# Linear attention, then a routed MoE on one core: the routing table moved into the attention, one dispatch per expert

## Chip, cores and metric

The kernel runs on one core of a Trainium2 chip. The metric is device time in microseconds, the median of several executions. Durations of single instructions come from one profiled execution, whose own time is given with its span.

## What is computed

The reference, cut to what matters:

```python
for t in range(S):                       # q, k, v, alpha: (4, 8, 768, 48), f32
    state = alpha[:, :, t, :, None] * state + einsum('bhd,bhe->bhde', k[:, :, t], v[:, :, t])
    y[:, :, t] = einsum('bhd,bhde->bhe', q[:, :, t], state)
x = y.transpose(0, 2, 1, 3).reshape(3072, 384)
...
xn = x / (norm(x) + 1e-6); en = emb / (norm(emb) + 1e-6)
logits = xn @ en.T / tau                 # 8 experts
expert_idx = argmax(logits, axis=1)
probs = exp(logits - max); probs /= probs.sum() + 1e-9
gate_w = probs[arange(N), expert_idx]
for e in range(8):                       # w1[e]: 384x1024, w2[e]: 1024x384
    h = maximum(x[mask] @ w1[e], 0)
    out[mask] = gate_w[mask, None] * (h @ w2[e])
```

With the reference's seeded inputs the experts get 418, 365, 379, 426, 395, 371, 351 and 367 of the 3072 rows.

## The kernel before

The work is in three stages, each with tile pools of its own. A scheduler orders the instructions on each engine from the program order and the tiles' dependencies, so an instruction can stand earlier than its line suggests; each engine then runs its own list strictly in order.

**Attention** (lines 95 to 399). The 4 x 768 tokens are 24 chunks of 128; six chunks make a sequence. The eight heads are padded to 64 columns and lie two to a 128-wide pair. The loop at L383 is a software pipeline over chunks s: `load` (L223, SP's queue: alpha, k, q, v, four buffers), `decays` (L233: PE turns alpha, k and q into pa, pk and pq, L216; DVE scans r at L246 and a at L260, and makes kr at L253 and qs at L266), `scores` (L317: PE's sc, which DVE masks into sm at L330), `keys_back` (L268: pkb, copied to kb by ACT), `update` (L295: PE's pd, which DVE adds to the decayed state at L315, or copies at L311 in the first chunk of a sequence), `decay_state` (POOL's dec, L287), `mix_states` and `mix_chunk` (PE's py, L340 and L352, copied to yT by ACT at L358) and `rows` (L360: PE's px at L365 turns rows back to tokens and gives the logits; ACT copies x at L367; DVE sums the logits lg at L368; SP's queue stores the row to `x_rows` in DRAM at L373; ACT sums the squares). In one pass, `rows` works on chunk s-3, `mix_chunk` on s-2, `update` on s-1 and `decays` on s. The PSUM tiles py, px and pd share one pool, `ps_mm`, of three buffers (tag "mm", L100); a buffer is free again when the last reader of its tile is done. The three turned tiles have three buffers, sc has one: seven of eight banks.

After each sequence `choose(b)` (L182) takes the largest normed logit and the gate of its 768 rows: ACT's Sqrt (L187) and Exp (L204), 13 small DVE instructions, and six POOL adds that count how many earlier chunks' rows each partition gave to each expert (L201).

**Routing table** (lines 402 to 488). It begins when all chunks are chosen. Two matmuls give each row its rank within its expert (rk, L408 and L411), DVE turns the ranks to places in 128-row blocks, L450 to L453 build `put` (token number and gate, spread over the block numbers), and 24 matmuls (inv, L458) invert the placing. The result is, for each of at most 31 blocks, which token to gather (gidx), where to scatter (sidx), the gate (bgate), the block's expert (eblk) and whether it needs new weights (fresh).

**Experts** (lines 491 to 577). `block(j)` (L504) reads the expert's number into a register of SP, loads the 1.5 MB w1 and w2 of that expert into the buffer of parity j (skipped where the block two before had the same expert), gathers 128 rows (L524, an indirect DMA from POOL's queue), turns them (pxg, xgT), runs 24 matmuls of 128 columns for the first layer (ph, L543), with ACT's Relu, and 8 of 384 columns for the second (pyo, L553), multiplies by the gate on DVE (L557) and scatters the rows (L558). 24 blocks stand in a row. The number of further ones is read into a register of every engine (L571), and a `Switch` at L575 branches to an arm with that many blocks; here it is three.

```python
        ps_mm = c1.enter_context(tc.tile_pool(name="ps_mm", bufs=3, space=PSUM))
...
        more = nc.values_load(
            nmore, min_val=0, max_val=NBLK - NS,
...
        for n in tc.Switch(more, NBLK - NS + 1):
            for j in range(NS, NS + n):
                block(j)
```

Of the kernel before, what the change touches and what calls it, by code (L numbers as in the profile page):

```python
# [15 lines left out]
SP = mybir.EngineType.SP  # L16

# [6 lines left out]
def kernel(  # L24
# [24 lines left out]

    NBLK = (N + E * (P - 1)) // P  # L50
    FAR = 1 << 20

    x_rows = nc.dram_tensor("x_rows", (N, DM), FP32, kind="Internal").ap()
# [14 lines left out]
    cols_i = consts.tile([P, P], I32)  # L68
    nc.gpsimd.iota(cols_i, pattern=[[1, P]], base=0, channel_multiplier=0)
    cols = consts.tile([P, P], FP32)  # L70
# [6 lines left out]
    nc.vector.tensor_scalar(first, cols[:, 0:E], -1.0, float(E), ALU.mult, ALU.add)  # L77


    lg = consts.tile([P, NS, E], FP32)  # L80
    sq = consts.tile([P, NS], FP32)
    gate = consts.tile([P, NS], FP32)
    chosen = consts.tile([P, NS, E], FP32)
    before = consts.tile([P, NS + 1, E], FP32)
    nc.gpsimd.memset(before[:, 0], 0.0)
    rtau = consts.tile([P, 1], FP32)
    gidx = consts.tile([P, NBLK], I32)
    sidx = consts.tile([P, NBLK], I32)
    bgate = consts.tile([P, NBLK], FP32)
    eblk = consts.tile([1, NBLK], I32)  # L90
    fresh = consts.tile([1, NBLK], I32)
    nmore = consts.tile([1, 1], I32)


    with ExitStack() as c1:
        pads = c1.enter_context(tc.tile_pool(name="pads", bufs=1))
        work = c1.enter_context(tc.tile_pool(name="work", bufs=2))
        ps_tr = c1.enter_context(tc.tile_pool(name="ps_tr", bufs=3, space=PSUM))
        ps_sc = c1.enter_context(tc.tile_pool(name="ps_sc", bufs=1, space=PSUM))
        ps_mm = c1.enter_context(tc.tile_pool(name="ps_mm", bufs=3, space=PSUM))  # L100
# [36 lines left out]
        sel = pads.tile([P, NP, 2 * D + E], FP32, name="sel")  # L137

        al0 = pads.tile([P, NP, NS], FP32, name="al0")

        def prepare():
# [15 lines left out]
            nc.vector.reciprocal(en, en)  # L157
            embp = work.tile([E, H, DP], FP32, name="embp", bufs=1)
# [23 lines left out]
        def choose(b):  # L182
            s0, s1 = b * NCH, (b + 1) * NCH
            shp = [P, NCH, E]
            l = lg[:, s0:s1]
            rn = work.tile([P, NCH], FP32, name="rn")
            nc.scalar.activation(rn, sq[:, s0:s1], AF.Sqrt)  # L187
            nc.vector.tensor_scalar(rn, rn, 1e-6, None, ALU.add)
            nc.vector.reciprocal(rn, rn)
            nc.vector.tensor_scalar(rn, rn, rtau, None, ALU.mult)  # L190
            nc.vector.tensor_tensor(l, l, bc(rn, shp, 2), ALU.mult)
            top = work.tile([P, NCH], FP32, name="top")
            nc.vector.tensor_reduce(top.unsqueeze(2), l, axis=AX.X, op=ALU.max)
            win = work.tile(shp, FP32, name="win")
            nc.vector.tensor_tensor(win, l, bc(top, shp, 2), ALU.is_equal)
            nc.vector.tensor_tensor(win, win, bc(first, shp, 1), ALU.mult)
            best = work.tile([P, NCH], FP32, name="best")
            nc.vector.tensor_reduce(best.unsqueeze(2), win, axis=AX.X, op=ALU.max)
            nc.vector.tensor_tensor(chosen[:, s0:s1], win, bc(best, shp, 2), ALU.is_equal)
            for s in range(s0, s1):  # L200
                nc.gpsimd.tensor_tensor(before[:, s + 1], before[:, s], chosen[:, s], ALU.add)  # L201
            sh = work.tile(shp, FP32, name="sh")
            nc.vector.tensor_tensor(sh, l, bc(top, shp, 2), ALU.subtract)
            nc.scalar.activation(sh, sh, AF.Exp)  # L204
            g = gate[:, s0:s1]
            nc.vector.tensor_reduce(g.unsqueeze(2), sh, axis=AX.X, op=ALU.add)
            nc.vector.tensor_scalar(g, g, 1e-9, None, ALU.add)
            nc.vector.reciprocal(g, g)
# [151 lines left out]
        def rows(s):  # L360
# [3 lines left out]
            for p in range(NP):  # L364
                nc.tensor.matmul(px[:, p], lhsT=yT[:, p], rhs=sel[:, p], start=True, stop=True)  # L365
            x = work.tile([P, NP, 2 * D], FP32, name="x", bufs=3)
            nc.scalar.copy(x, px[:, :, 0 : 2 * D])  # L367
            nc.vector.tensor_reduce(  # L368
                lg[:, s].unsqueeze(2), px[:, :, 2 * D :].rearrange("t p e -> t e p"),
                axis=AX.X, op=ALU.add,  # L370
            )
            xf = x.rearrange("t p d -> t (p d)")
            nc.sync.dma_start(out=x_rows[s * P : (s + 1) * P], in_=xf)  # L373
            x2 = work.tile([P, DM], FP32, name="x2")
            nc.scalar.activation(x2, xf, AF.Square, accum_out=sq[:, s : s + 1])
            if s % NCH == NCH - 1:
                choose(s // NCH)
# [22 lines left out]


    with ExitStack() as c2:
        rt = c2.enter_context(tc.tile_pool(name="rt", bufs=1))
        ps_rt = c2.enter_context(tc.tile_pool(name="ps_rt", bufs=1, space=PSUM))


        rk = ps_rt.tile([P, (NS + 1) * E], FP32, name="rk")
        nc.tensor.matmul(  # L408
            rk, lhsT=ones, rhs=before.rearrange("p s e -> p (s e)"), start=True, stop=False
        )  # L410
        nc.tensor.matmul(  # L411
            rk[:, 0 : NS * E], lhsT=earlier, rhs=chosen.rearrange("p s e -> p (s e)"),
            start=False, stop=True,
        )

        nb_i = rt.tile([P, E], I32, name="nb_i")
        nb = rt.tile([P, E], FP32, name="nb")
        start = rt.tile([P, E], FP32, name="start")
        row0 = rt.tile([P, E], FP32, name="row0")
        nc.vector.tensor_scalar(nb, rk[:, NS * E :], float(P - 1), None, ALU.add)  # L420
        nc.vector.tensor_copy(nb_i, nb)
        nc.vector.tensor_scalar(nb_i, nb_i, 7, None, ALU.arith_shift_right)
        nc.vector.tensor_copy(nb, nb_i)
        nc.vector.tensor_tensor_scan(start, nb, zeros[:, 0:E], 0.0, ALU.add, ALU.add)
        nc.vector.tensor_tensor(start, start, nb, ALU.subtract)
        nc.vector.tensor_scalar(row0, start, float(P), None, ALU.mult)


        shp = [P, NS, E]
        place = rt.tile(shp, FP32, name="place")  # L430
        nc.vector.tensor_tensor(
            place, rk[:, 0 : NS * E].rearrange("p (s e) -> p s e", e=E), bc(row0, shp, 1), ALU.add
        )
        nc.vector.tensor_tensor(place, place, chosen, ALU.mult)
        dest = rt.tile([P, NS], FP32, name="dest")
        nc.vector.tensor_reduce(dest.unsqueeze(2), place, axis=AX.X, op=ALU.add)
        dest_i = rt.tile([P, NS], I32, name="dest_i")
        nc.vector.tensor_copy(dest_i, dest)
        low_i = rt.tile([P, NS], I32, name="low_i")
        nc.vector.tensor_scalar(low_i, dest_i, P - 1, None, ALU.bitwise_and)  # L440
        low = rt.tile([P, NS], FP32, name="low")
        nc.vector.tensor_copy(low, low_i)
        nc.vector.tensor_scalar(dest_i, dest_i, 7, None, ALU.arith_shift_right)
        blk = rt.tile([P, NS], FP32, name="blk")
        nc.vector.tensor_copy(blk, dest_i)


# [43 lines left out]
    with ExitStack() as c3:  # L491
# [12 lines left out]
        def block(j):  # L504
# [28 lines left out]
            for i in range(KT):  # L533
                nc.tensor.transpose(px[:, i], xg[:, i * P : (i + 1) * P], ident)  # L534
# [73 lines left out]
```

## Time and profile before

| | us |
|---|---|
| median of 3 executions (lowest, highest) | 541.3 (540.84, 541.91) |
| the profiled execution: its time, its span | 542.78, 541.0 |
| last px matmul of the attention ends | 168.4 |
| first matmul of the first layer begins | 213.46 |
| busy in the span: PE, DVE, ACT, POOL | 465.5, 195.6, 98.0, 109.8 |
| from 100 to 170 us: PE, DVE, POOL busy | 62.0, 60.7, 17.4 |
| from 195 to 213 us: PE busy; DMA share, rate | 3.7; 0.90, 335 GB/s |

Times in the trace count from the span's start. "x" numbers are records; an fp32 matmul of the program leaves two matmul records and two weight-load records, a transpose one of each. A busy PE is not a PE at its peak. In the slices of the page each digit is the busy share in tenths of one fortieth of the span; PEclk is the granted clock of PE in tenths. The chain of waits lists, in order of time, what the end of the span hung on: "issue" is time in which an engine waited for nothing that the profile shows.

### The profile page before, as it was taken

Reading aid. Unit: us, or ns where it says so; the run is one execution under the profiler, and the core shown is the slowest. Engines: PE = TensorE matmul, PEld = TensorE weight load, DVE = VectorE, ACT = ScalarE, POOL = GpSimd, SP = SyncE. Lnnn points to the kernel's source line nnn. Section 1 sums busy time; section 2 is a strip of 40 time slices with the busy share of each in tenths; the row PEclk is TensorE's granted clock in tenths of the full one; section 3 lists DMA queues with packets and bytes.
Section 4 is the critical chain, followed back from the end, with each engine's and each line's share of the span. In section 5 each row is a group of like instructions: output and inputs, shape, how many; then the busy total and the mean of one; then the engine's idle time right before and its main releaser. Section 6 shows DMA issues by size and latency. Waiting matters only on the chain.

```text
span 541.0 us, 9273 instructions
## 1 busy us (share of the span) xinstructions
PE 465.5 (86%) x3677; PEld 388.2 (72%) x3677; DVE 195.6 (36%) x415; ACT 98.0 (18%) x190; POOL 109.8 (20%) x200
## 2 busy tenths in 40 slices
PE   2999999999884445999999999999999999963992
PEld 2898898888873334877787777877778777743871
DVE  5999999999993721000101011010110101101000
ACT  2142433533524000110011100111001100000110
POOL 6132331322221123000112022120221200102000
PEclk9999999999997555999999999999999999995997
DMA  9888877767010049109469294177149286583000
GB/s 186 168 177 191 175 160 155 158 147 153 26 45 29 1 154 394 50 20 323 161 205 334 82 328 160 54 269 247 45 158 321 91 288 208 163 294 101 16 16 17
DMA packets 130229, 84.78 MB, mean 157 GB/s; under 512 B 102095, under 2 KB 121595, under 8 KB 130168
## 3 DMA queue, kind: packets, MB, share of 16 engines
q1 hardware_dynamic: 126336, 73.93, 48.0%
q0 software_dynamic: 3456, 10.03, 5.1%
q8 instruction: 32, 0.52, 0.4%
q14 instruction: 29, 0.24, 0.1%
q10 hardware_dynamic: 376, 0.05, 0.1%
HBM read 109.17 MB, written 10.03 MB: 220 GB/s over the span
## 4 chain that ended last, share of the span: by engine, by line
PE 58%; DVE 23%; issue 12%; DMA 2%; another core or an unknown queue 1%; POOL 1%; ACT 1%; POOLq 0%; DVEq 0%; ACTq 0%
PE ph L543 25%; PE pyo L553 23%; DVE r L246 4%; DVE sm L330 4%; DVE a L260 4%; DVE kr L253 2%; PE inv L458 2%; DVE state L315 2%; PE sc L326 1%; DMA xg<-x_rows,gidx 1%; DVE qs L266 1%; PE px L365 1%; DVE xgT L536 1%; PE pkb L275 1%
## 5 line engine op out<-in xcount | busy, mean ns | idle before, releaser
L543 PEld LDWEIGHTS ph<-xgT,w 128*128 128x128 f32 x1296 | 151.6, 196 | 11.9 <-DVE xgT L536 7.9
L543 PE MATMUL ph<-xgT,w 128*128 128x128 f32 x1296 | 153.5, 279 | 5.5 <-DVE xgT L536 5.5
L553 PE MATMUL pyo<-w,hT 128*128 128x384 f32 x432 | 143.8, 486 | 0.0
L553 PEld LDWEIGHTS pyo<-w,hT 128*128 128x128 f32 x432 | 80.0, 190 | 50.1
L557 DVE TENSOR_SCALAR y<-pyo,bgate 128x384 f32<-128x384 f32 x27 | 16.7, 617 | 263.8 <-PE pyo L553 263.8
L549 ACT ACTIVATE hT<-ph 128x512 f32<-128x512 f32 x54 | 32.3, 597 | 321.2 <-PE ph L543 321.2
L558 POOL DMA_INDIRECT out_dram<-y,sidx x27 | 27.0, 1001 | 187.7 <-DVE y L557 185.3
L524 POOL DMA_INDIRECT xg<-x_rows,gidx x27 | 27.9, 1034 | 105.8 <-PE pxg L534 82.9
L534 PE MATMUL pxg<-ident,xg 128*128 128x128 f32 x81 | 14.6, 320 | 27.4 <-DMA xg<-x_rows,gidx 19.0
L287 POOL TENSOR_TENSOR dec<-state,end 64x256 f32<-64x256 f32 x40 | 24.4, 609 | 68.1 <-DVE state L315 45.9
L534 PEld LDWEIGHTS pxg<-ident,xg 128*128 128x128 f32 x81 | 10.9, 162 | 33.3 <-issue 30.6
L330 DVE TENSOR_TENSOR sm<-sc,causal 128x512 f32<-128x512 f32 x48 | 30.9, 678 | 0.3 <-PE sc L326 0.3
L326 PE MATMUL sc<-qs,kr 64*128 64x128 f32 x384 | 28.8, 291 | 1.7 <-DVE sm L330 1.4
L246 DVE TENSOR_TENSOR_SCAN r<-pa,inr 128x511 f32<-128x511 f32 x24 | 29.2, 1217 | 1.7 <-PE pa L216 1.2
L260 DVE TENSOR_TENSOR_SCAN a<-pa,ini 128x512 f32<-128x512 f32 x24 | 29.3, 1219 | 0.7
L536 DVE COPY xgT<-pxg 128x384 f32<-128x384 f32 x27 | 14.1, 550 | 42.1 <-PE pxg L534 23.0
L326 PEld LDWEIGHTS sc<-qs,kr 64*128 64x128 f32 x384 | 24.1, 193 | 6.0 <-DVE sm L330 2.7
L365 PE MATMUL px<-sel,yT 128*128 128x104 f32 x192 | 25.3, 275 | 0.7 <-ACT yT L358 0.7
L352 PE MATMUL py<-sm,vt 128*64 128x128 f32 x384 | 25.3, 274 | 0.0
L365 PEld LDWEIGHTS px<-sel,yT 128*128 128x128 f32 x192 | 23.3, 192 | 1.2 <-ACT yT L358 0.9
L358 ACT COPY yT<-py 128x512 f32<-128x512 f32 x24 | 14.1, 586 | 53.7 <-PE py L352 53.7
L340 PE MATMUL py<-qs,dec 128*128 128x128 f32 x160 | 21.6, 278 | 0.0
(126 smaller groups left out, 370.6 us busy)
## 6 DMA issues: line engine op xcount, KB each, us to landing
w<-in_moe_w_dram SPq DMA_DIRECT2D x54, 1536.0 KB
at<-in_alpha_dram SPq DMA_DIRECT2D x24, 192.0 KB
kt<-in_k_dram SPq DMA_DIRECT2D x24, 192.0 KB
qt<-in_q_dram SPq DMA_DIRECT2D x24, 192.0 KB
vt<-in_v_dram SPq DMA_DIRECT2D x24, 192.0 KB
x_rows<-x SPq DMA_DIRECT2D x24, 192.0 KB
xg<-x_rows,gidx POOLq DMA_INDIRECT x27, 4.9
out_dram<-y,sidx POOLq DMA_INDIRECT x27, 5.7
```

The costliest lines, as they stand in the source:

```text
L246: nc.vector.tensor_tensor_scan(r[:, L - 2 :: -1], pa[:, L - 1 : 0 : -1], inr[:, L - 2 :: -1], 1.0, ALU.mult, ALU.add,)
L260: nc.vector.tensor_tensor_scan(a, pa, ini, 0.0, ALU.mult, ALU.add)
L326: nc.tensor.matmul(sc[:, hh, p], lhsT=kr[sl, p], rhs=qs[sl, p], start=True, stop=True)
L330: nc.vector.tensor_tensor(sm[:, hh], sc[:, hh], causal.to_broadcast([P, NP, P]), ALU.mult)
L352: nc.tensor.matmul(py[DP * hh : DP * hh + DP, p], lhsT=vt[:, 2 * p + hh], rhs=sm[:, hh, p], start=("dec" not in d and p == 0), stop=True, ...
L365: nc.tensor.matmul(px[:, p], lhsT=yT[:, p], rhs=sel[:, p], start=True, stop=True)
L524: nc.gpsimd.indirect_dma_start(out=xg, out_offset=None, in_=x_rows, in_offset=bass.IndirectOffsetOnAxis(ap=gidx[:, j : j + 1], axis=0), bo ...
L534: nc.tensor.transpose(px[:, i], xg[:, i * P : (i + 1) * P], ident)
L543: nc.tensor.matmul(ph[:, f], lhsT=w1_t[:, i, (f0 + f) * P : (f0 + f + 1) * P], rhs=xgT[:, i], start=(i == 0), stop=(i == KT - 1),)
L549: nc.scalar.activation(hT[:, f0 : f0 + 4], ph, AF.Relu)
L553: nc.tensor.matmul(py, lhsT=hT[:, f], rhs=w2_t[:, f], start=(f == 0), stop=(f == FT - 1))
L558: ins = nc.gpsimd.indirect_dma_start(out=out, out_offset=bass.IndirectOffsetOnAxis(ap=sidx[:, j : j + 1], axis=0), in_=y, in_offset=None, ...
```

## The change

What leaves: the whole routing stage after the attention, `choose`, the gates in the table, the weights' registers and conditions, the 128-row blocks as the unit of the expert stage, the `Switch` for the last blocks.

What comes:

- `place(g)` in place of `choose(b)`. The chunks are cut into six groups (five, five, five, five, three, one). After a group's last `rows`, DVE picks the experts, POOL (for the last group DVE) adds up `before`, PE ranks the group's rows (rk), DVE finds each row's place, and per chunk POOL makes in_row and put (L257 and L259 of the changed kernel), which PE adds to the table inv (192 columns: 24 possible blocks for each of eight experts). inv stays in a PSUM bank of its own through the attention (`ps_iv`); `ps_mm`, which py, px, pd and rk share, has two buffers instead of three.
- `tables()` after the loop makes gidx, sidx and the number of 64-row halves of each expert.
- A row of `x_rows` also holds the eight logits and the norm (393 columns instead of 384). The gates are computed from the gathered rows (`gates`).
- Weights have three buffers each, for the whole kernel. The first three experts' loads stand in the loop and depend on nothing; those of expert e+3 follow after expert e.
- Per expert one `Switch` over ten arms by its number m of halves (0 to 8, or more than 512 rows, which loops over blocks). An arm gathers for expert e+2, runs the first layer over all m x 64 rows at once (24 matmuls of up to 512 columns), turns the rows of expert e+1 between them, and runs the second layer by 128-row block; an odd half at the end is computed as two half-sums in the two halves of the PSUM partitions. `tc.switch_hint` at the head of an arm names the register of the next dispatch, for PE, ACT, DVE and POOL.

```diff
-        ps_mm = c1.enter_context(tc.tile_pool(name="ps_mm", bufs=3, space=PSUM))
+        ps_iv = c1.enter_context(tc.tile_pool(name="ps_iv", bufs=1, space=PSUM))
+        ps_mm = c1.enter_context(tc.tile_pool(name="ps_mm", bufs=2, space=PSUM))
...
+        def place(g):
...
+            for s in range(s0, s1):
+                eng.tensor_tensor(before[:, s + 1], before[:, s], chosen[:, s], ALU.add)
+            rk = ps_mm.tile([P, GMAX, E], FP32, tag="mm", name="rk")[:, 0:n]
...
+            for s in range(s0, s1):
+                i = s - s0
+                in_row = work.tile([P, P], FP32, name="in_row")
+                eng.tensor_scalar(in_row, cols[:, 0:P], low[:, i : i + 1], None, ALU.is_equal)
+                put = work.tile([P, E * NB], FP32, name="put")
+                eng.tensor_scalar(
+                    put, cols, blk[:, i : i + 1], toks[:, s : s + 1], ALU.is_equal, ALU.mult
+                )
+                nc.tensor.matmul(
+                    inv, lhsT=in_row, rhs=put, start=(s == 0), stop=(s == NS - 1),
+                    skip_group_check=True,
+                )
...
+            if s == NS:
+                for e in range(NW):
+                    weights(e)
+        tables()
...
+        def arm(e, m):
...
+            if e + 1 < E:
+                tc.switch_hint({g: count[e + 1] for g in hinted}, 2 * NC + 2, label=f"expert{e + 1}")
+            if e + 2 < E:
+                gathers(e + 2)
+            hT = hp.tile([P, FT, NC * P], FP32, name="hT") if m else None
+            for f in range(FT):
+                if m:
+                    first_layer(w1_t, hT, xT, f, m * HALF)
+                if e + 1 < E and f % 2 == 1:
+                    prepare(e + 1, f // 2)
+            if e + 1 < E:
+                gates(xg_s[(e + 1) % NXG], gt_s[(e + 1) % 2], NC)
+            for t in range((m + 1) // 2):
+                j = e * NB + t
+                second_layer(
+                    w2_t, hT, t, min(P, m * HALF - t * P), gt[:, t : t + 1], sidx[:, j : j + 1]
+                )
...
+        for e in range(E):
+            for m in tc.Switch(count[e], 2 * NC + 2, hint=f"expert{e}"):
+                if m <= 2 * NC:
+                    arm(e, m)
+                else:
+                    many(e)
+            if e + NW < E:
+                weights(e + NW)
```

## Prediction

> **What bounds the kernel now.** I read the page's slices first, then the windows by stage, the chain of waits, and the timeline of one attention step and of the Switch. Slices (13.5 us each): PE busy tenths and granted clock, from which I cut the stages.
>
> ```profile
> PE   2999999999884445999999999999999999963992
> PEclk9999999999997555999999999999999999995997
> ```
>
> The span is 541.0 us, of a profiled execution of 542.78 us; the median shown is 541.3. I sum changes in the profiled execution and take them off the median. Three stages: attention to 168.4 us (end of the last px matmul), the table and first loads to 213.46 (first ph), the experts to 530.95 (last pyo) with a tail of 10.0.
>
> One attention step, from the timeline (start, duration, instruction):
>
> ```profile
> 117.47 0.69 PE L303 MATMUL pd<-vt,kb 128*64 128x64 f32 x16
> 119.96 1.04 PE L365 MATMUL px<-sel,yT 128*128 128x104 f32 x8
> 122.30 0.87 DVE L315 TENSOR_TENSOR state<-pd,dec 64x256 f32<-64x256 f32 x2
> 123.20 0.19 DVE L368 TENSOR_REDUCE lg<-px 128x8 f32<-128x32 f32 x1
> 123.42 1.22 DVE L246 TENSOR_TENSOR_SCAN r<-pa,inr 128x511 f32<-128x511 f32 x1
> ```
>
> DVE sets the 6.4 us step (r began at 117.04, the next at 123.42): r 1.22, kr 0.69, ini 0.17, a 1.22, qs 0.69, sm 1.28, state 0.87, lg 0.19. PE runs ahead: px is done 1.3 us before state has read pd. Three PSUM tiles are in use at that time: pd, px and the next py.
>
> Then the chain of waits across the join of the stages (start, length, what):
>
> ```profile
> 184.42 10.52 PE inv L458 x48
> 195.68 7.67 issue
> 203.35 2.44 PE pxg L534 x9
> 205.80 6.65 DMA xg<-x_rows,gidx
> ...
> 213.46 7.30 PE ph L543 x48
> 220.76 5.16 PE pyo L553 x16
> 225.93 5.36 PE ph L543 x48
> ```
>
> Here nothing but the table, then the first two weight sets with the gathers behind them, holds PE for 45.1 us (168.4 to 213.46). In the expert stage PE is the bound: 24 fp32 matmuls of 128 columns (48 records) take 5.36 us, 0.1117 a record; 8 of 384 columns (16 records) take 5.16, 0.3225 a record. The first block after the idle stretch takes 1.9 more (clock 0.5).
>
> The one Switch is at 482 us. PE's sequencer there (count, durations in ns, first and last start):
>
> ```profile
> L571 PEldq TENSOR_LOAD <-nmore x1: 486/486/486, 477.9 to 477.9; - x1
> ...
> L603 PEldq COMPARE_BRANCH  x2: 337/3126/5914, 478.8 to 526.5; - x2
> ```
>
> The branch into the Switch took 5.91 us; the one out of it, for which the arm had issued a prefetch hint, took 0.34. PE's sequencer reached the load 4.4 us before its matmuls ended (482.33), so it works that far ahead. After it PE still stood until 497.57, since the gathers were issued behind the branch.
>
> **Part 1, attention: +30 us.** (a) The pool of py, px and pd goes from 3 to 2 buffers, to free a bank for inv. In the built order of the changed kernel 16 px matmuls wait for DVE's state of the step before (it empties the bank), and 2 more for the copy that starts a sequence. The wait stands ahead of the rest of pa, pk and pq on PE, and DVE's lg and next r wait for those. Walk from the end of state, T: px needs 1.15 from first load to last result (167.26 to 168.40, where it waited too), two more pa transposes 0.22, hand-over 0.1: r starts at T+1.5, instead of T+0.26 (123.16 to 123.42). That is 1.2 a step, and PE's own work (about 6.6 to its next px) does not exceed the new 7.6 us. 18 x 1.2 = 21.6. Ends: 0, if the wait falls while PE is busy anyway, and 18 x 1.5 = 27.
> (b) The table. Out: choose, 13 DVE instructions of 0.2 us four times (three in the loop, 8 us). In: place, 12 of them per group, four groups in the loop (9.6): +1.6. Its matmuls: rk, and per chunk an inv of 192 columns, 2 x 192/128 x 0.11 = 0.33; 20 in the loop make 6.6, which fit into PE's new waits. But the pairs in_row and put run on POOL, no row of which has the shape: 0.19 for a 128x128 memset and 0.6 for 192 of put's 2.96 ns a column (L453, 2.2 us for 744) are the ends; I take 0.35 and 0.5, the middle, as the operation is simpler than L453's and reads more than a memset. Two buffers make the third pair wait for the first inv, and in the order inv stands among the sc matmuls, whose result sm waits for. A group is thus dec 0.65, memset 0.5, five pairs 4.3, lg 0.2, after state, against 3.9 of DVE work before sm: some 1.5 late, plus 0.8 for rk behind five adds of 0.27 on POOL. 4 x 2.3 - 1 (waits of choose) + 1.6 is about +9; ends 0 and +18. I take +8, since the steps of two groups don't pay (a).
> (c) The first three weight sets (six loads of 1.5 MB) are drawn forward on SP's queue between the q, k, v and alpha loads. At 335 GB/s (195 to 213 us) they are 28 us of the 16 engines; those were busy 0.77 from 66 to 100 us and 0.40 from 100 to 170, so 50 us are free there. The last alpha load landed by 132, for use at 154. I take 0. Without that cover POOL's memset waits for alpha, with dec behind it: at most 4 us. ACT gets 24 Sqrt of 0.21 and loses six table loads of 1.28; it is busy 28 of 70 us. 0.
>
> **Part 2, from the last px to the first ph: 45.1 becomes 21.5, -23.6 us.** lg 0.25; its copy on POOL 0.25; five choice steps 1.1; add 0.2; rk 0.6; seven steps 1.5, with six counts between them 0.9; in_row and put on DVE 0.65; inv 0.45; tok and gidx 0.45: 6.4. Four gathers start 1.3 apart; one from start to PE takes 3.2 (491.32 to 494.55): 0.2 + 3.9 + 3.2 = 7.3. Transposes 0.5, two register loads 1.0, the unhinted first branch 5.9, rest 0.4. The weights landed long before. Ends: 16 (branch hidden) and 27.
>
> **Part 3, experts: 317.5 becomes 276, -41 us.** The reference's inputs give experts 418, 365, 379, 426, 395, 371, 351 and 367 rows: 27 blocks as in the trace, or 7, 6, 6, 7, 7, 6, 6, 6 halves (51). The loop for more than 512 is not entered. First layer: six halves 48 x 0.3225 = 15.5, seven 48 x 448/384 x 0.3225 = 18.1. Second: three full blocks 15.5; a half runs as 16 records in two column groups, and py at L352, split likewise, took 0.88 for 16 where full ones take 1.79: 2.6. Sum 5 x 31.0 + 3 x 36.1 = 263.2 (before 27 x 10.5 = 284). Transposes in the arms 7 x 12 x 0.11 = 9.2. Clock after the idle stretch 1.9. Seven further dispatches: load 0.5 and two hinted branches of 0.34 fit into the 4.4 us lead of PE's sequencer; after a half, lead 2.6, too; I give 0.3 each, 2 in all. What else leaves: the 15.3 us at the old Switch and 0.5 us of xgT waits per pair of blocks. The second layer's scatters, gates and next transposes hide under PE; late next would be ACT, whose Exp for the next gates stands before the relus and waits for DVE to enter the arm. PE has four ph buffers, 7.7 us of cover.
>
> Against this stands the Trainium skill, "Runtime: NRT & Kernel Launch", Instruction fetch mechanics: prefetch is sequential, and a taken branch out of the window of two pages stalls for a fetch, so unrolled code is preferred. The 5.91 us row is that; the 0.34 us row is not. By the rule alone each of the seven dispatches would pay for two fetches, and the sum would be that of the second rival below.
>
> Sum: +30 - 23.6 - 41 = -34.6; 541.3 - 34.6 = **507 us**.
>
> **Rivals.**
> - *Half the hints miss.* One cold branch per dispatch: 0.5 + 0.34 + 5.91 - 4.4 = 2.4 us on PE, seven times 17, so 522 to 524. For it: no row shows a hint whose target depends on a register. Against: 0.34.
> - *Dispatch costs more than it saves (slower).* Both branches miss on every engine: 7 x (2 x 5.91 + 0.5 - 4.4) = 55 us on PE, and the clock falls in the gaps (1.6 us for the block after the Switch, 6.92 instead of 5.36): 11 more. 507 + 53 to 66 gives 560 to 573. It decides from (541.3 - 507)/7 = 4.9 us per dispatch. For it: 5.7 us and more on all engines at the one Switch; against: the hinted exit.
> - *The attention does not slow* (the buffers are enough, POOL keeps up): without (a) and most of (b), 507 - 25 = 482. Against: px and pd overlap in time in every step shown.
> - That the change does not do what it says would be the loop for many rows; the counts exclude it.
>
> **Chances.** Forecast (492 to 516): 0.55; half the hints miss (516 to 540): 0.20; no slower attention (475 to 492): 0.12; dispatch dearer: 0.13. The range 487 to 540 leaves out the slower case and part of the fast one. A measurement tells 0.2% from no change: faster 0.86, same 0.01, slower 0.13.
>
> **What would show it.** Attention: DVE idle of 1.2 before lg with PE px as releaser, steps of 7.6, the last px near 198. First ph near 220. ph records of 0.32 and 0.38, no gap over 1 us between the last pyo of an expert and the next ph, COMPARE_BRANCH on PE at 0.3. I am wrong if that gap is 5 us and more, or if steps stay at 6.4.

## The result and the profile after

The changed kernel takes 599.55 us (median of 4 runs, 596.93 to 602.40), the kernel before 541.21 (4 runs, 540.84 to 541.91): 1.108 times as long, 95% interval 1.103 to 1.113. The forecast was 507. The profiled execution took 600.01 us; its span is 598.2. Cut into stages at the same instructions as before (the first ph matmul of the kernel before starts at 213.25 in the timeline; the chain of waits counts it from 213.46):

| stage (us) | before | forecast | after |
|---|---|---|---|
| start to end of last px | 168.4 | 198 | 239.6 |
| last px to first ph | 44.9 | 21.5 | 25.3 |
| first ph to last pyo | 317.7 | 276 | 322.7 |
| tail | 10.1 | 10.0 | 10.6 |

The join of the stages is shorter by 19.6 us, near the forecast, but the attention grew by 71 and the experts by 5. The slices of the page (15 us each, busy tenths of PE and its clock) show both:

```profile
PE   2889598698788869359959969799779959899992
...
PEclk9999879969969978559989989979969969999997
```

The dips of the first 16 slices are new (there PE had nearly only nines), and so is the fall in about every third slice of the experts, each with a fall of the clock at it or behind it. One step without a table, from the timeline (start, duration, instruction, idle time before it and what ended it):

```profile
195.16 0.87 DVE L391 TENSOR_TENSOR state<-pd,dec 64x256 f32<-64x256 f32 x2
...
196.08 1.14 PE L441 MATMUL px<-sel,yT 128*128 128x104 f32 x8 [0.93 <-DVE state L391]
...
197.31 0.19 DVE L445 TENSOR_REDUCE x<-px 128x8 f32<-128x32 f32 x1 [1.28 <-issue]
197.54 1.22 DVE L322 TENSOR_TENSOR_SCAN r<-pa,inr 128x511 f32<-128x511 f32 x1
```

This is step (a) of the forecast as it was walked: px waits for state, DVE idles 1.28 before the sum of the logits, and r starts 7.64 us after the r before it (189.90). Now a step with a group of the table:

```profile
119.94 1.00 POOL L259 TENSOR_SCALAR put<-cols,blk,toks 128x192 f32<-128x192 f32 x1
120.93 0.59 POOL L257 TENSOR_SCALAR in_row<-cols,low 128x128 f32<-128x128 f32 x1
...
120.99 1.01 PE L262 MATMUL inv<-put,in_row 128*128 128x192 f32 x2 [0.65 <-POOL put L259]
121.51 1.00 POOL L259 TENSOR_SCALAR put<-cols,blk,toks 128x192 f32<-128x192 f32 x1
...
123.36 0.59 PE L441 MATMUL px<-sel,yT 128*128 128x104 f32 x2
...
124.05 0.19 DVE L445 TENSOR_REDUCE x<-px 128x8 f32<-128x32 f32 x1 [8.30 <-PE px L441]
```

POOL needs 1.6 us for each pair of in_row and put, and the five pairs of a group stand together. The inv matmuls are in the middle of px and pa in PE's order, so PE goes on at POOL's pace; px, begun at 115.90, ends after 123.36, and DVE, which sets the step, stands still for 8.30 us. From r to r this step takes 18.73 us where before it took 5.37. PE's granted clock is 0.62 from 117 to 125 us (an inv takes 1.01 there, the first of the group took 0.59); over the attention it is 0.90, before 1.00.

In the experts, PE's sequencer shows the second surprise. Each dispatch has two branches: the entry, from the Switch into an arm, and the exit, from the end of the arm to the code behind the Switch. A branch of 2 us and more is called cold here, against some 0.3 us for one that is not. The lead is the time by which the sequencer runs ahead of PE's matmuls. All branches on PE together (count, shortest, median and longest in ns):

```profile
L688 PEldq COMPARE_BRANCH  x16: 315/3814/5274, 259.9 to 581.8; - x16
```

Of 16 branches only one took 0.3 us: the exit from the last arm. The other seven exits took 3.25 to 4.02, the entries 2.31 to 5.27. PE stood 34.0 us in all between an expert's last pyo and the next ph (called gaps below), and the first 12 records behind the five longer gaps took 12.0 us more than they do at full clock.

### The profile page after: what moved, and what is told of

It reads as the page before. It is cut to its first block, busy times and chain, and to the rows that moved or that the text cites. A ratio compares the mean times of both kernels' runs of the same rounds, so it can differ in the third digit from the quotient of the medians.

```text
span 598.2 us, 7873 instructions
## 1 busy us (share of the span) xinstructions
PE 486.0 (81%) x2802; PEld 327.9 (55%) x2802; DVE 203.2 (34%) x470; ACT 96.5 (16%) x221; POOL 152.1 (25%) x272
## 5 line engine op out<-in xcount | busy, mean ns | idle before, releaser
L552 PE MATMUL ph<-xT,w 128*128 128x384 f32 (+1 forms) x384 | 150.9, 548 | 39.4 <-issue 36.5
L552 PEld LDWEIGHTS ph<-xT,w 128*128 128x128 f32 x384 | 77.1, 207 | 101.2 <-issue 76.2
L564 PE MATMUL pyo<-w,hT 128*128 128x384 f32 x384 | 125.2, 486 | 0.0
L564 PEld LDWEIGHTS pyo<-w,hT 128*128 128x128 f32 x384 | 72.4, 190 | 49.0
L568 DVE TENSOR_SCALAR y<-pyo,gt 128x384 f32<-128x384 f32 x24 | 14.8, 618 | 126.5 <-PE pyo L564 126.5
L530 DVE COPY xT<-pxg 128x384 f32<-128x384 f32 x32 | 17.8, 555 | 104.3 <-PE pxg L529 99.5
L556 ACT ACTIVATE hT<-ph 128x384 f32<-128x384 f32 (+1 forms) x64 | 32.4, 509 | 116.6 <-PE ph L552 112.9
L262 PE MATMUL inv<-put,in_row 128*128 128x192 f32 x48 | 21.1, 536 | 18.9 <-POOL put L259 17.1
L262 PEld LDWEIGHTS inv<-put,in_row 128*128 128x128 f32 x48 | 10.4, 270 | 26.1 <-POOL put L259 24.3
L450 ACT COPY x<-px 128x384 f32<-128x384 f32 x24 | 11.5, 479 | 81.2 <-DVE x L445 73.4
```

The source lines that it names most:

```text
L262: nc.tensor.matmul(inv, lhsT=in_row, rhs=put, start=(s == 0), stop=(s == NS - 1), skip_group_check=True,)
L552: nc.tensor.matmul(ph, lhsT=w1_t[:, i, f * P : (f + 1) * P], rhs=xT[:, i, 0:n], start=(i == 0), stop=(i == KT - 1),)
L556: nc.scalar.activation(hT[:, f, 0:n], ph, AF.Relu)
L564: nc.tensor.matmul(py, lhsT=hT[:, f, t * P : (t + 1) * P], rhs=w2_t[:, f], start=(f == 0), stop=(f == FT - 1),)
```

## Experiments

The theory after the result: two buffers cost what was forecast; the table's lumps on POOL cost the rest of the attention; and the hint for the next Switch (L592) takes the place of the hint that each arm has for its own exit, so that every dispatch pays two cold branches. Rivals stand in the expectations.

### The attention

**Two buffers alone**, in the kernel before (before_two_banks):

```diff
-  ps_mm = c1.enter_context(tc.tile_pool(name="ps_mm", bufs=3, space=PSUM))
+  ps_mm = c1.enter_context(tc.tile_pool(name="ps_mm", bufs=2, space=PSUM))
```

> The kernel before, with the pool of py, px and pd cut from three PSUM buffers to two and nothing else changed: the term (a) of the first part alone. Theory: px must wait until DVE has emptied the bank of pd into state, and r of the next step starts 1.2 to 1.3 us later, so the steps in the middle of a sequence go from 6.4 to 7.6 us (the record of the changed kernel shows 7.64) and the attention ends 18 to 24 us later: 560 to 566 us. Rival: the 7.64 us steps of the changed kernel come from the weights drawn forward on the queue of loads or from the shared POOL work, and two buffers are enough: 541 to 545 us, steps of 6.4.

558.06 us, ratio 1.029 (1.027 to 1.031), a little under what was expected. The last px ends at 184.3 instead of 168.4: +15.9. Its timeline has the wait of the changed kernel:

```profile
124.96 0.86 DVE L315 TENSOR_TENSOR state<-pd,dec 64x256 f32<-64x256 f32 x2
...
125.88 1.14 PE L365 MATMUL px<-sel,yT 128*128 128x104 f32 x8 [0.86 <-DVE state L315]
```

The steps are 7.58 long, against 7.64 with the weights drawn forward, so these cost nothing that can be seen here. The sum came out under the 18 to 24 expected: the two intervals that begin a sequence do not change (5.59 and 8.19 in both). What the table adds in the changed kernel is the rest, 239.6 - 184.3 = 55.3 us.

**The pairs on DVE** (table_dve):

```diff
-  eng.tensor_scalar(in_row, ...); eng.tensor_scalar(put, ...)
+  nc.vector.tensor_scalar(in_row, ...); nc.vector.tensor_scalar(put, ...)
```

> The changed kernel with in_row and put on DVE instead of POOL, everything else as it is (adds of the counts stay on POOL). Theory: the inv matmuls stand in order on PE and each waits for a put that POOL takes 1.6 us a chunk to make, which costs the four steps with a group 45 to 53 us; on DVE a chunk should be about 0.65 us, so a group costs 3.3 us of DVE instead of 13, and the clock no longer falls: 560 to 572 us, last px at 200 to 212. Rival: the stall comes from the place of inv in PE's order and from rk, whoever makes put: 590 to 600 us.

572.69 us, 26.9 less than the changed kernel, just outside what was expected; the last px ends at 213.8. The same two operations, first on POOL in the changed kernel, then on DVE here (count, shortest, median and longest in ns):

```profile
L257 POOL TENSOR_SCALAR in_row<-cols,low x23: 589/599/614, 69.5 to 243.2; 128x128 f32<-128x128 f32 x23
...
L259 POOL TENSOR_SCALAR put<-cols,blk,toks x23: 991/1008/1012, 70.9 to 243.8; 128x192 f32<-128x192 f32 x23
```

```profile
L257 DVE TENSOR_SCALAR in_row<-cols,low x24: 255/278/507, 68.6 to 218.4; 128x128 f32<-128x128 f32 x24
...
L259 DVE TENSOR_SCALAR put<-cols,blk,toks x24: 367/374/379, 68.8 to 218.6; 128x192 f32<-128x192 f32 x24
```

So POOL's pace was half of the 55 us. The steps with the second to fourth group still take 12.4 to 13.2 us; in this kernel PE waits 10.8 us for POOL's five adds ahead of rk, with DVE's next operation behind rk.

**One pair a step**, still on POOL (spread_put):

```diff
-  for s in range(s0, s1): in_row, put on POOL; inv
+  pend.append((s, low, blk))        # in place()
+  with tc.issue_after(dec): in_row, put of one chunk    # once a step
+  with tc.issue_after(px): inv of the pair of the step before
```

> The changed kernel (599.6 us, with its hints and dispatches) with in_row and put still on POOL, but one chunk in each step, issued behind dec, and its inv one step later behind px; the last four chunks on DVE. Theory: what costs 45 to 53 us in the four steps with a group is that five chunks of 1.6 us stand together while PE waits in order at inv; POOL's own time is free in a step of 7.6 us (it has some 2 to 3 us of other work), so nearly all of it goes: 550 to 565 us, the last px at 185 to 200. Rival: POOL at 1.6 us a chunk more is late with dec and the next alpha every step, so the cost is only spread: 580 to 600.

573.49 us, ratio 1.058 (1.056 to 1.060), last px at 216.8: as good as DVE and no better, short of what was expected. So the lumps were a little under half of the 55 us. What stays, by elimination, goes with the choice itself (its 12 small operations, the adds, rk). Where part of that goes became clear in a later kernel that has three buffers and the choice cut in two (whole3, below):

```profile
90.15 1.00 POOL L219 TENSOR_SCALAR put<-cols,blk,toks 128x192 f32<-128x192 f32 x1
...
91.10 0.18 POOL L497 COPY lg<-x 128x8 f32<-128x8 f32 x1
91.32 0.20 DVE L254 TENSOR_REDUCE top<-lg 128x5 f32<-128x40 f32 x1 [2.62 <-POOL lg L497]
```

DVE makes the logits, POOL copies them for the choice, and DVE waits 2.62 us for a copy of 0.18, which stands behind in_row and put. What the removal of this copy from DVE's path is worth was measured later (the sixth form).

### The dispatch

**No Switch at all** (fixed_counts):

```diff
-  for m in tc.Switch(count[e], 2 * NC + 2, hint=f"expert{e}"): ...
+  arm(e, (7, 6, 6, 7, 7, 6, 6, 6)[e])
```

> The changed kernel without Switch, register loads and hints: the numbers of halves 7, 6, 6, 7, 7, 6, 6, 6 are written into the program, so the dispatch on the counts is left out (it is right for these inputs alone). Theory: the dispatch costs the expert stage all that it is longer than the 276 us of the forecast, so first ph to last pyo is 272 to 280 us, the first ph comes 4 to 5 us sooner, and the whole takes 545 to 555 us. Rival: part of the stage's surplus is something else (the late gathers, loads of weights, the half clock after the attention): the stage stays over 290 us and the whole over 562.

544.24 us, ratio 1.004 (1.002 to 1.006). The experts take 274.4 us: the work of part 3 was forecast right (276), and the dispatches cost 322.7 - 274.4 = 48.3 us. The code that is fetched shows in the table of DMA queues (packets, MB, share of 16 engines), the changed kernel's first, then this one's:

```profile
q14 instruction: 116, 0.95, 0.5%
q8 instruction: 43, 0.70, 0.5%
```

```profile
q8 instruction: 22, 0.36, 0.3%
q14 instruction: 13, 0.11, 0.1%
```

The changed kernel fetches 1.65 MB of code, this one 0.47.

**No hints** (no_hint):

```diff
-  tc.switch_hint({g: count[e + 1] for g in hinted}, 2 * NC + 2, label=f"expert{e + 1}")
-  for m in tc.Switch(count[e], 2 * NC + 2, hint=f"expert{e}"):
+  for m in tc.Switch(count[e], 2 * NC + 2):
```

> The changed kernel without the switch hints in the arms (the Switch has no hint label, its arms are the same). Theory: the hint for the next Switch takes the place of the hint that the arm has for its own exit, so the hinted program pays for both branches; without it the exit takes 0.3 us again as at the last arm (0.32), the entry stays at 4 to 6 us, most of which lies in the lead of PE's sequencer (5.8 us after a full block, 2.6 after a half): the gaps before the seven later experts shrink from 34 us in all to under 12, and 2 us each of half clock go with them: 560 to 580 us. Rival 1: the hints do shorten something and the entries become as dear as the first (5.9) with exits still at 3.7: 600 to 610. Rival 2: PE hits cold code whatever is hinted, since the arms lie far apart: 598 to 602, same.

585.85 us, 13.7 less than the changed kernel, under half of what was expected. The exit of expert 1 (six halves), in the changed kernel and here:

```profile
L688 PEldq COMPARE_BRANCH  x1: 3529/3529/3529, 341.0 to 341.0; - x1
```

```profile
L684 PEldq COMPARE_BRANCH  x1: 315/315/315, 339.3 to 339.3; - x1
```

The exits took 0.31 from every arm for six halves, but 3.43 to 4.19 from the three for seven. So the second hint had taken the exit's place, and something else does so in the longer arms. Counted in the built program (a weight load and a matmul for each record, with waits, hint and branch), an arm for six is 227 or 228 instructions long on PE, one for seven 258 or 259.

**Shorter arms** (short_arm): the three transposes of the fourth block go behind the Switch.

```diff
-  prepare(e + 1, f // 2)     # in the arm, four blocks
+  prepare(e + 1, f // 2)     # in the arm, three blocks
   ...
+  prepare(e + 1, NC - 1)     # behind the Switch
```

> The kernel without the switch hints (585.85 us), and the three transposes of the next expert's fourth block moved out of the arms to behind the Switch, so that the arm for seven halves is about 252 instructions long on PE instead of 258. Without the hints the exit took 0.31 us from the arms for six halves (about 228 instructions) and 3.4 to 4.2 from those for seven. Theory: the chip holds the branch's target beside the code that runs only while the arm is within 256 instructions, so all eight exits now take 0.3, the gaps after the three arms for seven fall from 8 us to 3 to 4, and the first layers behind them run at full clock: 564 to 573 us. Rival: the exit is lost because of what the seventh half itself does (its matmuls in column groups, its lead of 2.6 us), not for the length: exits stay at 3.4 to 4.2 and the time at 583 to 588.

595.6 us, so the time missed both theories, but all eight exits took 0.31 to 0.33. What was lost is the lead: the entry branch of expert 2 starts 0.6 us before expert 1's last pyo ends (343.16, 343.80), where it had 4.7 us without the transposes there (340.39, 345.06). PE's waits name DVE's xT (10.4 us): the transposes stand behind DVE's part of the arm.

**A hint behind the Switch** (hint_behind), in the same kernel:

```diff
+  tc.switch_hint({g: count[e + 1] for g in hinted}, ...)    # behind the Switch
   prepare(e + 1, NC - 1)
```

> As the kernel with the short arms, and the hint for the next Switch is back, but it stands behind the Switch before it (behind the exit, ahead of the register load) instead of at the head of the arm. Theory: it no longer takes the place of the exit's hint, so the exits stay at 0.3; but it stands only 0.6 to 1.0 us ahead of its branch, so the entry falls from 5 us by no more than 1: within 4 us of the kernel with the short arms. Rival 1: the hint makes the entry cheap as well (0.3): all gaps vanish, 548 to 556. Rival 2: a hint here again costs the exits: over 580.

593.6 us, which tells nothing of a hint in that place: the scheduler had drawn all seven hints ahead of the first dispatch. It does show that hints which do not stand in the arms leave the exits alone (0.31 for all eight) and that the entries gain nothing from hints so far ahead (3.28 to 6.45). The same question was asked again at the end (entry_hint).

**Weights later** (late_weights, from no_hint):

```diff
-  if e + NW < E: weights(e + NW)               # behind the Switch
+  if 1 <= e <= E - NW: weights(e - 1 + NW)     # head of the next arm
```

> The kernel without the switch hints (585.85 us), with the loads of the weights for experts 3 to 7 issued at the head of the next arm instead of straight behind the Switch. In every kernel so far the entries into experts 1 to 5, at whose moment such a load has just begun, took 1.5 to 2 us longer (5.0 to 6.2 us here) than those into 6 and 7, where none is left (4.1). Theory: fetching the arm's code shares the transfers with the weights, so with the loads later the five entries fall to about 4 and the time by 5 x 1.7 = 8 us, less what the sequencer's lead hid: 576 to 582 us. Rival: the later entries are shorter for another reason (no gathers in front of them, or their place in the program): entries stay at 5 to 6 and the time at 584 to 588.

593.38 us. It did not move the first load, which started at 300.9 (299.8 in no_hint), as its buffer comes free then; it only drew the second one to it, from 311.2 to 303.6. So it does not decide. The deciding run leaves the loads out (no_reload: `weights(e + NW)` deleted), so that experts 3 to 7 are computed with the weights of experts 0, 1, 2, 0 and 1; its time is for comparison alone:

> The kernel without the switch hints (585.85 us), with the loads of the weights of experts 3 to 7 left out, so that these experts are computed with the weights of experts 0, 1, 2, 0 and 1. Issuing the loads behind the next dispatch did not move them (their buffers come free at the same moment either way, and the first load still started at the exit), so that run told nothing; this one does. Theory: the entries into experts 1 to 5 are 1.5 to 2 us longer than those into 6 and 7 because the code is fetched through the transfers that the weights have just filled: without the loads all entries take 4 to 4.3 us, and the time is 576 to 582. Rival: entries 1 to 5 stay at 5 to 6.2: the difference lies elsewhere, 583 to 587.

577.95 us, and the entries into experts 1 to 5 took 3.92 to 4.31 instead of 5.04 to 6.21. The theory holds: with a load of weights just begun, these entries take 1.0 to 2.1 us longer.

### All together

**First form** (all_mended): three buffers again, as inv is summed in a tile of that pool and added up by DVE; besides, one pair a step, short arms, no hints in them, and the half block first.

```diff
-  inv = ps_iv.tile(...)                 # own bank, ps_mm bufs=2
+  iv = ps_mm.tile(..., tag="mm")        # per group, ps_mm bufs=3
+  nc.vector.tensor_tensor(inv_s, inv_s, iv, ALU.add)
-  for t in range((m + 1) // 2): second_layer(...)
+  for t in reversed(range((m + 1) // 2)): second_layer(...)
```

> All terms taken away together, still the whole computation: inv is summed group by group in a tile of the pool of py, px and pd (three buffers again) and added up in the on-chip memory by DVE; one chunk of in_row and put in each step; no hints in the arms, one before the first dispatch alone; short arms; in the second layer the half block goes first, so that PE's sequencer has a full lead at the exit. By the theory the attention ends at 172 to 180, the first ph comes 20 to 24 us later, the experts take 280 to 290 with gaps of 0 to 1.5 us, the tail 10: 485 to 505 us. Rival: one of the three terms was not what it was taken for, and its part stays: 515 to 545.

545.16 us, ratio 1.006 (1.004 to 1.009): the upper end of the rival's range. The steps are 6.4 again, but those with a group 10 to 13.6, and the transposes behind the Switch take the lead as in the kernel with short arms (gaps of 25.3 us).

**Second and third form:** the choice is cut in two; the transposes behind the Switch get a PSUM tile of their own (whole2), or are back in the arms (whole3).

```diff
-  place(g): choose; adds; rk; at, row, low, blk; pairs      # in one go
+  place(g): choose; adds behind dec
+  rank(g): rk behind px of the next step
+  spread(g): at, row, low, blk behind sm of the next step; pairs one a step
```

> The kernel with all terms taken away (545.2 us) in a second form, the whole computation: no hints; the choice for a group is cut in two, so that DVE does not wait for the rank matmul within the step (the adds behind dec, the rank behind px of the next step, its use behind sm); the three transposes of the fourth block still stand behind the Switch, but in a PSUM tile of their own, so that they wait for nothing of the arm just left; half block first. Theory: the gaps were 25 us since the transposes behind the Switch waited for DVE's last y and took the sequencer's lead away: exit 0.3, 1.1 to the branch, entry 5, against a lead of 5.8 gives gaps of 0.5 to 1.5, 3 to 10 in all, and no half clock behind them: the experts 278 to 288 us instead of 311. In the attention the four steps with a group lose another 3 to 5 us each: 502 to 518. Rival: the transposes still wait for something behind the Switch: the experts stay over 300 us, the whole over 525.

> As the kernel of the second form in the attention, without hints and with the half block first, but with all transposes in the arms (those for seven halves are 258 instructions long again) and the weights issued at the head of the next arm. Theory: the exits from the three arms for seven are lost (3.5 to 4), and with the full lead of 5.8 their gaps are 3.5 to 5 each; the other four nearly vanish: 12 to 18 us of gaps, the experts 285 to 295 us: 508 to 525. Rival: if the loads do not matter for the entry, 5 us more.

547.89 and 535.51 us, both above what was expected; the third is the first whole form that takes less time than the kernel before, by 1% (0.989, 0.985 to 0.993). In the second the transposes still waited for DVE (10.7 us in the experts): its rival was right. In the third the three exits from arms for seven were cold again (3.27 to 3.62), and entries 1 to 5, behind the loads at the head of the next arm, took 5.59 to 7.23: the experts took 309.0 us where 285 to 295 were expected.

**Arms of known length** (whole4, 5, 6, 7): hT kept for all experts, which takes waits out of the arms, and the weights loaded from ACT's queue behind the second first-layer tile of the next arm.

```diff
-  hT = hp.tile([P, FT, NC * P], FP32, name="hT")
+  hT = hT_s[e % 2]
+  with tc.issue_after(relu of f == 1): nc.scalar.dma_start(w1), (w2) of e - 1 + NW
```

> As the fourth whole form, but with two PSUM tiles for the transposes and four for the first layer, as in the changed kernel: by the built program the arm for seven halves is 256 instructions long on PE for expert 0 and 257 for experts 3 and 4. Theory: the limit is a block of 256 instructions that the arm must not leave: the exit of expert 0 takes 0.3 and those of 3 and 4 over 3 us, 515 to 525 us. Rival: the limit is somewhere between 252 and 255, and all three are slow; or above 257, and all are fast.

> As the third whole form (535.5 us), with two changes. The tiles of hT are kept for all experts and the transposes have four PSUM tiles of their own (the first layer two), which takes waits out of the arms: by the built program an arm for seven halves is 254 or 255 instructions long on PE, all transposes included. And the weights are loaded from ACT's queue, two first-layer tiles into the next arm, so the loads no longer start at the exit. Theory: all exits take 0.3, entries about 4: 5.4 us for a dispatch, within the lead of 5.8, so that the seven gaps fall from 20 us to under 4 and no half clock follows them: 510 to 520 us. Rival: exits from arms for seven stay at 3.3 to 3.6 (the limit is not 256): 526 to 532.

> As the fourth whole form, and DVE's sum of the logits goes straight to the tile that the choice reads, POOL copying it from there into the row that is stored. In the third whole form the choice waited 2.7 us a group for POOL's copy, which stood behind in_row and put. Theory: the steps with a choice fall from 9.1 to 9.6 us to about 7, four or five times: 8 to 13 us less than the fourth form, 498 to 510 us. Rival: the choice's own small operations on DVE are what the steps cost, and the gain is under 4 us.

The fifth form takes 515.93 us. Its three exits from arms for seven, the first from an arm of 256 instructions on PE, the other two from arms of 257:

```profile
L753 PEldq COMPARE_BRANCH  x1: 326/326/326, 249.3 to 249.3; - x1
...
L753 PEldq COMPARE_BRANCH  x1: 3472/3472/3472, 352.4 to 352.4; - x1
...
L753 PEldq COMPARE_BRANCH  x1: 3792/3792/3792, 395.0 to 395.0; - x1
```

So in these arms the step lies between 256 and 257 instructions. It is not shown that a longer arm always loses its exit: all cold exits with one hint came from arms of 257 to 259, while the arm for three blocks in the kernel before is 412 instructions long by the same count, has its hint at the head (484.7 us) and left in 0.34 (526.5 us). The later seven entries took 3.99 to 4.36. The fourth (545.21) and sixth (533.93) have no cold exit and no gap, and were slower than expected by a wait of their own making, here in the fourth (us in total, times, longest):

```profile
PE ph L612 <- ACT hT L616: 25.2, 6, 4.6
```

They had two PSUM tiles of the first layer instead of four. ACT enters the arm with its Exp, which waits for DVE, and PE ran out of tiles before the first relu; with four, in the fifth, this wait is 0.3 in all. The sixth form has one more edit, and it gave about what was expected, last px at 182.9 instead of 196.7:

```diff
-  DVE: x[:, LG : LG + E] <- px;  POOL: lg_g[g][:, s - s0] <- x
+  DVE: lg_g[g][:, s - s0] <- px;  POOL: x[:, LG : LG + E] <- lg_g
```

The seventh form joins this attention to the expert stage of the fifth, with arms for seven of 255 (expert 0) and 256 instructions (experts 3 and 4):

> The attention of the sixth whole form (first ph at 202 us) with the expert stage of the fifth (four PSUM tiles for the first layer, two for the transposes), hT kept and first touched by DVE, so that by the built program the arms for seven halves are 255 (expert 0) and 256 instructions long on PE. In the fourth and sixth form the gaps at the dispatches were gone, but ACT came into the arm 4 us after PE and two tiles of the first layer did not cover that (ph waited 25 us for hT). Theory: first ph at 202, all exits 0.3, entries 4, gaps under 1 us but for one wait of 3.5 for the gates in the first expert, the experts 278 to 283 us, the tail 10.6: 490 to 500 us. Rival: an arm of 256 is already too long in some places (the fifth form showed one of 256 that fitted): two exits stay cold, 499 to 506.

**493.94 us, ratio 0.912 (0.910 to 0.915)** to the kernel before. All exits 0.31 to 0.33, no gap behind a dispatch, 277.7 us for the experts, against 276 forecast and 274.4 without any Switch:

```profile
L753 PEldq COMPARE_BRANCH  x16: 311/2136/4422, 198.3 to 474.8; - x16
```

```profile
PE   0999999899899882599999999999999999999991
...
PEclk9999999999899996599999999999999999999997
```

The median of the branches lies between the exits (0.3) and the entries (about 4), which PE's lead now hides; the slices have lost their dips but for the join.

> The seventh whole form (493.9 us) with PE's instructions of the expert stage kept in the order they are written, and on PE alone a hint for the next dispatch between the exit of one arm and the register's use (in the earlier kernel that was to try this, all seven hints had been drawn ahead of the first dispatch, so it told nothing). By the built program it stands behind the register load and directly ahead of the branch's own four instructions. Theory: it starts the fetch no sooner than 0.3 to 0.5 us ahead of the branch, so entries stay at 3.5 to 4.2 us and exits at 0.31; the gaps were gone already, so the time stays within 3 us of 493.9. Rival 1: a hint with the target in a register does its work at once: entries at 0.3. Rival 2: it costs the exits also here: exits at 3.5, 510 to 520 us.

The last run puts the hint where hint_behind had meant it, and keeps PE's instructions in the order they are written:

```diff
+  with tc.manual_schedule(engines={PE}):
     for e in range(E):
         for m in tc.Switch(count[e], ...): ...
+        tc.switch_hint({PE: count[e + 1]}, ...)    # behind the Switch
```

493.96 us. With the hint 0.4 us ahead of the branch, the entries behind a hint took 3.46 to 3.93 us instead of 3.95 to 4.25, on the mean 3.6 instead of 4.1, so they were shorter by about the time the hint had. One profiled execution of each stands behind this, and the order on PE changed with it: a hint with its target in a register seems to work, but in this place it has no time to.

The seven dispatches, from the traces (us):

| kernel | exits, six / seven halves | entries 1 to 5 | entries 6, 7 | gaps | experts |
|---|---|---|---|---|---|
| changed | 3.25-4.02 all | 4.16-5.27 | 2.31, 2.70 | 34.0 | 322.7 |
| no_hint | 0.31 / 3.43-4.19 | 5.04-6.21 | 4.08, 4.12 | 26.4 | 309.1 |
| no_reload | 0.31 / 3.35-3.66 | 3.92-4.31 | 3.97, 4.11 | 18.2 | 301.3 |
| whole5 | 0.32 / 0.33, 3.47, 3.79 | 3.99-4.19 | 4.06, 4.36 | 6.3 | 287.7 |
| whole7 | 0.31-0.33 all | 3.95-4.15 | 4.25, 4.08 | 0 | 277.7 |
| fixed_counts | none | none | none | 0 | 274.4 |

## Why the prediction was wrong

- **1(a), two buffers, +21.6:** right in mechanism and place (steps of 7.6, px behind state); measured alone +15.9, as the intervals that begin a sequence did not grow. (In the step shown there px is done 1.3 us before state begins, and 2.2 before it has read pd.)
- **1(b), the table, +8 (ends 0 and +18): failed.** Measured 55.3. (Its own terms give 9.8, and with 5.6 - 3.9 = 1.7 for the lateness some 10.6, not 9; this is small beside the miss.) The price of put was bounded by 0.6 us from another operation's cost per column; it took 1.01, and in_row 0.60 instead of 0.35, so that a group is 8 us on POOL and not 4.3. Worse was the step behind it. I took a late put to delay sm by the difference; but inv stood in PE's order ahead of px and pa too, which DVE's next step needs, so each lump of POOL's time fell on the path nearly whole, and the half clock came on top. That the matmuls "fit into PE's new waits" counted PE's time and not its order. Spreading the pairs, or giving them to DVE, took 23 to 26 us of it away; in the last form the whole table costs the attention 182.7 - 168.4 = 14.3, after the sixth form's edit, which moved POOL's copy off DVE's path, had taken 13.8 off the fourth (196.7 to 182.9).
- **1(c), weights, 0:** right as far as it shows (steps of 7.64 with them, 7.58 without).
- **Part 2, 21.5:** nearly (25.3), in part by luck: the first branch took 4.2 and not 5.9, while the rest was longer, as the three chunks of the fifth group on POOL stood ahead of the last choice. With all pairs on DVE (table_dve) this stage took 21.3, with a first branch of 3.9.
- **Part 3, the work, 276:** right (274.4 with fixed counts).
- **Part 3, "seven further dispatches ... 2 in all": failed.** Measured 48.3: 34.0 of gaps, 12.0 of half clock behind them, 1.3 in the first expert (39.9 from its first ph to its last pyo, 38.6 with fixed counts). I took the hinted exit of 0.34 at the one Switch for the price of every hinted branch. That row had one hint in flight. With two, the exits lost theirs and the entries gained little; both branches missed, as in the second rival, which has 55 us of gaps and 11 of clock for it, where 34.0 and 12.0 were measured. The Trainium skill, "Runtime: NRT & Kernel Launch", Instruction fetch mechanics, which the text set against the change, has the code refilled in blocks of 256 instructions and a window of two of them. The exits from arms of 256 (0.33) and 257 (3.47, 3.79) agree with the size of a block; that the window is two blocks no run here shows.
- **Sum:** 507 + 41.6 (attention) + 3.8 (join) + 46.7 (experts) = 599.1; measured 599.55. The range left out the second rival, and no case had the attention beyond the ends of (a) and (b), 27 + 18 = 45, where it grew by 71.2.

Not settled: why, with the hints in, the entries into experts 6 and 7 took only 2.3 and 2.7; why the hinted exit from 412 instructions was not cold while those from 257 to 259 were, and what arms in between do; and what of the 14.3 us in the last form's attention could still go.

## What to carry to other kernels

A price read from one row holds for the state in which the row stood: the hinted exit of 0.34 had no second hint beside it, and an arm of another length. On an in-order engine, ask of an inserted operation what stands behind it, before asking whether its time fits. A design that loses may be sound: with its dispatches' branches within PE's lead and its table spread, this one takes 8.8% less time than the kernel before.

## What the runs showed of the hardware

- A second prefetch hint, issued on PE behind the one for the exit, costs the first: exits took 3.25 to 4.02 us, and 0.31 without it (arms for six halves). The traces fit one hint per engine, the last one issued.
- One instruction more can make a hinted exit cold: arms for seven halves of 251 to 256 instructions on PE gave 0.30 to 0.33 us, those of 257 to 259 gave 3.27 to 4.19. It is no limit on length as such: an arm of 412 gave 0.34.
- A cold branch into an arm took about 4 us on PE, up to 7.2 where a load of 1.5 MB had just begun (whole3). At 4 us it hid behind PE's lead of 5.8 us (from the exit to the end of the last pyo, 18 records of 0.32, in whole7), where nothing waited between.
- The same tensor_scalar takes POOL 0.60 and 1.01 us (128x128 and 128x192) and DVE 0.28 and 0.37.
